# Spreading projections and VectorE chains around an attention's exponentials

## The chip, the cores and the metric

One core of a Trainium2 chip. The time is the device's time for one execution in microseconds (us). The runs came from more than one chip, so each kernel is judged by its ratio to the kernel before in the same rounds on the same chip: the mean time of one kernel's fast runs over that of the other's, so not quite the ratio of the medians quoted.

## The reference, cut to what matters

Two independent halves, put side by side in the output. Half B is attention with 32 heads of 20 over 2048 tokens:

```python
qkv = (x @ wqkv).reshape(B, S, 3, H, Dh)        # S = 2048, H = 32, Dh = 20
p = softmax(einsum("bhqd,bhkd->bhqk", q, k) * scale)
o = einsum("bhqk,bhkd->bhqd", p, v);  out_b = o.reshape(B, S, D) @ wo
```

Half A is a convolution over the sequence (an FFT in the reference, sums of small matmuls in the kernel):

```python
kv = shift_conv(k, 4 taps) * v
out_a = q * (long_conv(kv, ssm_k) + kv * ssm_D)
```

## The kernel before

The program is written as one loop of 512 steps: four passes over query chunks, eight groups of four heads, sixteen key blocks. A step exponentiates one block on ScalarE while TensorE makes the next scores:

```python
for b in range(NB):                 # 512
    EXP_task(b)                     # 2 ACTIVATEs of 128x1024 on ScalarE
    S_task(b + 1)                   # 4 score matmuls
    PV_task(b - 1)                  # 4 value matmuls
    budget = 1.0
    if b >= 24 and b % 5 == 0: kv_task(...)   # 8 VectorE instructions at once
    if lock is None: ...run_best()  # the task with the earliest deadline
    if nm == 0 and conv: ...        # else pieces of the convolution, up to the budget
```

Everything else is fitted in as tasks: K, Q and V projections, N (transpose and normalise one head group), T (transpose for the output projection) and O (output projection). After the first steps all of them, and the convolution, write one spare PSUM bank, MISC, which a VectorE cast must empty before the next may start. In these traces the instructions of an engine run in the order they were queued, so a task that waits holds back the scores queued after it. A "handover" is the stretch where a pass is over and its T and O tasks run.

```python
def kv_task(tb):                    # half A: shift convolution of one block
    P.op("dve", ... tA = k0 * C0)
    for j in range(1, KS):
        P.op("dve", ... tB = kj * Cj);  P.op("dve", ... tA = tA + tB)
    P.op("dve", ... kvst = tA * v)   # then two stores and the next load
...
add(b + 10, 0.35, ("N", qc, g), ...)
add(b0 + 12, 0.4, ("T", qc, qt), ...)             # all four T at once
add(b0 + 16 + 8 * qt + 4 * hf, 0.7, ("O", qc, qt, hf), ...)
# OnT_task(qt >= 2) first runs both O tasks of qt - 2
```

The softmax here doesn't subtract the row's maximum and nothing guards it: scores larger than these inputs give would overflow.

## Time and profile before

| | us |
|---|---|
| median of the three runs made before the prediction | 1092.08 |
| span of the profiled run | 1093.4 |
| first exponential starts | 16.87 |
| stream of 1024 exponentials at their pitch, the time from one to the next without a wait (1024 x 0.9175) | 939.5 |
| lost inside the stream | 121.9 |
| after the last exponential (1093.4-1078.27) | 15.1 |

The rows of ScalarE's timeline are start, duration, engine, line, what it does and how many were merged, and in brackets the idle time before the group with what ended it. A group's duration is about (count-1) times the pitch plus one full instruction of 1.0 us; what is missing between groups is what ScalarE waited. Every microsecond of wait in that stream lengthens the kernel by one. The prediction shows the lines.

### The profile page before, as it was taken

What the parts mean: (1) busy time and instruction counts of PE and PEld (TensorE: products, weight loads), DVE (VectorE), ACT (ScalarE), POOL (GpSimd) and SP (SyncE); (2) the same over time, 40 slices, a digit from 0 to 9 for tenths busy, and PEclk for the clock granted to TensorE, in tenths of its full rate; (3) what the DMA queues carried; (4) which work ended last, traced back from release to release, by engine and by line L of the source; (5) the groups of instructions that cost most, each with busy time, mean ns of one, the idle gap of its engine ahead of it and who ended that gap; (6) DMA issues with size and microseconds to landing.
All of it is one profiled execution on the core that took longest, in us unless ns stands there. A gap on an engine that the chain in (4) does not pass through costs nothing.

```text
span 1093.4 us, 24833 instructions
## 1 busy us (share of the span) xinstructions
PE 850.1 (78%) x11264; PEld 393.5 (36%) x11264; DVE 273.7 (25%) x558; ACT 953.2 (87%) x1027; POOL 118.8 (11%) x97
## 2 busy tenths in 40 slices
PE   5887777776668888888877889888888966666666
PEld 3322222221123555555544455555554411111112
DVE  3345554555102111111112440111112132000002
ACT  3786766669996999999979699999998899999994
POOL 3000000000310111222111011222110000000000
PEclk9998988886556999999988899999997865555556
DMA  9102222223823488888898497788885321000000
GB/s 340 38 32 85 85 85 85 85 82 100 134 45 92 117 199 177 193 180 180 181 194 184 136 239 173 178 185 191 175 182 132 83 73 49 1 1 1 1 1 25
DMA packets 74758, 129.04 MB, mean 118 GB/s; under 512 B 25730, under 2 KB 51452, under 8 KB 74652
## 3 DMA queue, kind: packets, MB, share of 16 engines
q1 hardware_dynamic: 71979, 124.09, 47.8%
q0 software_dynamic: 704, 2.74, 0.6%
q8 instruction: 88, 1.44, 0.6%
q10 hardware_dynamic: 1968, 0.61, 0.2%
q14 instruction: 19, 0.15, 0.1%
HBM read 116.81 MB, written 13.23 MB: 119 GB/s over the span
## 4 chain that ended last, share of the span: by engine, by line
ACT 62%; PE 23%; DVE 11%; DMA 2%; issue 1%; SPq 0%; ACTq 0%
ACT P_sb L419 62%; PE PS L306 7%; PE PS L407 4%; PE PS L584 3%; PE PS L503 3%; PE PS L432 3%; PE PS L325 2%; DVE KT L313 2%; DVE R L357 2%; DVE R L355 2%; DVE QT L313 1%; DVE V_sb L330 1%; DMA R<-in_B_wqkv_dram 1%; DVE OT_sb L440 1%; DMA R<-kv_scratch 1%
## 5 line engine op out<-in xcount | busy, mean ns | idle before, releaser
L419 ACT ACTIVATE P_sb<-PS 128x1024 bf16<-128x1024 f32 x1024 | 950.5, 1145 | 119.2 <-PE PS L407 112.6
L407 PE MATMUL PS<-QT,KT 20*128 20x512 bf16 x2048 | 240.5, 459 | 150.9 <-ACT P_sb L419 145.0
L432 PE MATMUL PS<-P_sb,V_sb 128*21 128x512 bf16 x2048 | 239.1, 459 | 1.2 <-ACT P_sb L419 1.2
L584 PE MATMUL PS<-R 128*128 128x128 bf16 (+15 forms) x5120 | 220.4, 196 | 6.1 <-DMA R<-kext_scratch 4.3
L584 PEld LDWEIGHTS PS<-R 128*128 128x128 bf16 x5120 | 197.2, 99 | 53.2 <-issue 48.7
L407 PEld LDWEIGHTS PS<-QT,KT 20*128 20x128 bf16 x2048 | 53.2, 94 | 301.0 <-ACT P_sb L419 254.4
L561 POOL COPY R<-R 32x512 bf16<-32x512 bf16 x80 | 106.7, 1333 | 417.7 <-PE PS L584 405.1
L306 PE MATMUL PS<-R 128*20 128x512 bf16 x1280 | 94.0, 430 | 37.1 <-DVE KT L313 11.1
L432 PEld LDWEIGHTS PS<-P_sb,V_sb 128*21 128x21 bf16 x2048 | 50.7, 90 | 153.7 <-issue 151.3
L440 DVE CAST OT_sb<-PS 128x512 bf16<-128x512 f32 x32 | 22.1, 691 | 273.6 <-PE PS L432 273.6
L597 DVE CAST ZH<-PS 128x256 bf16<-128x256 f32 x40 | 17.0, 424 | 289.3 <-PE PS L584 289.3
L306 PEld LDWEIGHTS PS<-R 128*20 128x20 bf16 x1280 | 29.9, 98 | 82.6 <-DVE QT L313 19.1
L503 PE MATMUL PS<-Wo_sb,OnT 128*128 128x320 bf16 x160 | 37.4, 388 | 7.3 <-DVE Bout L507 3.8
L325 PE MATMUL PS<-R 128*128 128x160 bf16 (+1 forms) x160 | 29.1, 316 | 13.7 <-DVE KT L313 5.8
L313 DVE CAST KT<-PS 128x512 bf16<-128x512 f32 x32 | 22.1, 690 | 44.5 <-PE PS L306 44.5
L313 DVE CAST QT<-PS 128x512 bf16<-128x512 f32 x32 | 22.1, 690 | 43.7 <-PE PS L306 43.7
L538 POOL MEMSET R<- 128x2048 bf16 x2 | 3.6, 1805 | 267.1 <-DMA kvr_scratch<-R 267.1
L503 PEld LDWEIGHTS PS<-Wo_sb,OnT 128*128 128x128 bf16 x160 | 16.6, 118 | 25.3 <-DVE Bout L507 9.1
L507 DVE CAST Bout<-PS 128x320 bf16<-128x320 f32 x32 | 15.7, 491 | 37.7 <-PE PS L503 37.2
L453 PE MATMUL PS<-ident,OT_sb 128*128 128x128 bf16 x128 | 14.7, 246 | 13.1 <-DVE OT_sb L440 12.8
L357 DVE TENSOR_TENSOR R<-R 128x640 bf16<-128x640 bf16 x48 | 23.6, 492 | 1.6
L355 DVE TENSOR_TENSOR R<-R 128x640 bf16<-128x640 bf16 x48 | 23.5, 490 | 1.1
(44 smaller groups left out, 239.4 us busy)
## 6 DMA issues: line engine op xcount, KB each, us to landing
R<-kext_scratch SPq DMA_DIRECT2D x320, 264.0 KB, 5.6
R<-in_A_k_dram SPq DMA_DIRECT2D x15, 640.0 KB, 3.9
R<-in_B_x_dram SPq DMA_DIRECT2D x4, 640.0 KB, 7.4
kext_scratch<-in_A_ssm_k_dram POOLq DMA_DIRECT2D x1, 2560.0 KB, 13.7
R<-in_A_v_dram SPq DMA_DIRECT2D x16, 160.0 KB, 5.4
kv_scratch<-R SPq DMA_DIRECT2D x16, 160.0 KB
kvr_scratch<-R SPq DMA_DIRECT2D x16, 160.0 KB
R<-kvr_scratch SPq DMA_DIRECT2D x8, 320.0 KB, 7.3
```

The source lines that it names most:

```text
L306: ins = e.matmul(bank[bk][32 * i:32 * i + DH, :], W_sb[:, cc, off + i * DH:off + (i + 1) * DH], xT[:, cc, c * 512:(c + 1) * 512], start=(c ...
L313: P.op("dve", lambda e: e.tensor_copy(dstT[:, g, c * 512:(c + 1) * 512], bank[bk]), reads=[bkb[bk]], writes=[bd])
L325: ins = e.matmul(bank[bk][:, 0:w], xT[:, cc, kb * 128:(kb + 1) * 128], W_sb[:, cc, 2 * D + h0 * DH:2 * D + h0 * DH + w], start=(cc == 0), ...
L355: P.op("dve", lambda e, j=j: e.tensor_tensor(tB, k[:, j, :], Ctile[:, j, :], ALU.mult), reads=[b_kst[i], b_C], writes=[b_tB])
L357: P.op("dve", lambda e: e.tensor_tensor(tA, tA, tB, ALU.add), reads=[b_tA, b_tB], writes=[b_tA])
L407: ins = e.matmul(bank[bk], KT[32 * u:32 * u + DH, g, kb * 128:(kb + 1) * 128], QT[32 * u:32 * u + DH, g, qc * 512:(qc + 1) * 512], start=T ...
L419: P.op("act", lambda e, pr=pr, s0=s0: e.activation(P_sb[:, pr % NPS, :], PS[:, s0 * 512:s0 * 512 + 1024], ACT.Exp, scale=scale), reads=[bk ...
L432: ins = e.matmul(bank[OBANK][32 * u:32 * u + DH + 1, :], V_sb[:, kb, 4 * g + u, :], P_sb[:, (2 * b + u // 2) % NPS, (u % 2) * 512:(u % 2) ...
L440: P.op("dve", lambda e: e.tensor_copy(OT_sb[:, i, :], bank[OBANK]), reads=[bkb[OBANK]], writes=[b_OT[i]])
L503: ins = e.matmul(bank[bk][:, 0:320], OnT[:, i, cc, :], Wo_sb[:, cc, hf * 320:(hf + 1) * 320], start=(cc == 0), stop=(cc == NCC - 1))
L561: P.op("pool", lambda e, dst=dst, src=src: e.tensor_copy(dst, src), reads=[cv["KVr"]], writes=[cv["KVX"][i]] if X == 3 else [], extra=(cv[ ...
L584: P.op("pe", lambda e, o=o, lhsT=lhsT, rhs=rhs, st=st, last=last: e.matmul(o, lhsT, rhs, start=st, stop=last, skip_group_check=True), read ...
```

## The change

Four things: the Q buffer shrinks to two query chunks, each projected one pass ahead (so x and Wq get a place of their own and outlive the first pass); the kv and output chains of half A become generators that queue two VectorE instructions a step; tasks and convolution draw on a running balance (0.9 a step, 1.4 in the first 24) instead of 1.0 reset each step; new deadlines for N, T and O. In the tail, casts alternate between VectorE and ScalarE.

```diff
-        QT = sb("QT", [128, NG, S])
+        QT = sb("QT", [128, 2, NG, 512])
...
+        xT = sb("xT", [128, NCC, S])
+        WQ = sb("WQ", [128, NCC, D])
         R = sb("R", [128, max(ph0, ph1)])     # holds WK, WV first, the convolution later
...
-                add(b + 10, 0.35, ("N", qc, g), lambda: N_task(qc, g))
+                add(b + 4, 0.35, ("N", qc, g), lambda: N_task(qc, g))
...
-                    add(b0 + 12, 0.4, ("T", qc, qt), ...)
+                    add(b0 + 5 + 4 * qt, 0.4, ("T", qc, qt), ...)
-                        add(b0 + 16 + 8 * qt + 4 * hf, 0.7, ("O", qc, qt, hf), ...)
+                        add(b0 + 6 + 4 * qt + hf, 0.75, ("O", qc, qt, hf), ...)
...
-            allx = b_xT + [b_Wa, b_Wb] + b_xst + ...   # what the convolution's loads wait for
+            allx = [b_Wa, b_Wb] + b_xst + ...
...
+            for qc in range(1, 4):
+                add(128 * (qc - 1) + 70 + 6 * g, 1.25, ("Q", g, qc), ...)
...
-            budget = 1.0
-            if b >= 24 and b % 5 == 0 and kv_next[0] < NKB:
-                kv_task(kv_next[0])
+            bal = min(bal + (1.4 if b < 24 else 0.9), 1.2)
+            if conv is None and kv_over and not any(e[3][0] in "XKV" for e in pend):
+                conv_setup()
+                conv = conv_iter()
...
+            if b >= 6:
+                micro(2)
```

V's second task (480 columns) is also cut into one of 160 and one of 320.

## The prediction

> **What bounds the kernel now.** I read the page first, then ScalarE's timeline, then VectorE, TensorE, GpSimd and SyncE in the stretches where ScalarE stands still.
>
> ```profile
> PE 850.1 (78%) x11264; PEld 393.5 (36%) x11264; DVE 273.7 (25%) x558; ACT 953.2 (87%) x1027; POOL 118.8 (11%) x97
> ...
> ACT  3786766669996999999979699999998899999994
> ...
> L419 ACT ACTIVATE P_sb<-PS 128x1024 bf16<-128x1024 f32 x1024 | 950.5, 1145 | 119.2 <-PE PS L407 112.6
> ```
>
> ScalarE is the bound: 1024 exponentials, and what it waits for is the score matmul (L407). The slices show where: tenths of 6 to 8 in the first nine slices, then nearly full with three dips. ScalarE's timeline has the pitch and the gaps (start, duration, merged count, idle before):
>
> ```profile
> 89.26 9.84 ACT L419 ACTIVATE P_sb<-PS 128x1024 bf16<-128x1024 f32 x10 [3.81 <-PE PS L407]
> ...
> 215.52 10.15 ACT L419 ACTIVATE P_sb<-PS 128x1024 bf16<-128x1024 f32 x10 [3.89 <-PE PS L407]
> 229.57 9.75 ACT L419 ACTIVATE P_sb<-PS 128x1024 bf16<-128x1024 f32 x10 [3.90 <-PE PS L407]
> ...
> 606.75 1.94 ACT L419 ACTIVATE P_sb<-PS 128x1024 bf16<-128x1024 f32 x2 [7.45 <-PE PS L407]
> ...
> 903.00 29.44 ACT L419 ACTIVATE P_sb<-PS 128x1024 bf16<-128x1024 f32 x32 [0.46 <-PE PS L407]
> ...
> 1052.50 25.77 ACT L419 ACTIVATE P_sb<-PS 128x1024 bf16<-128x1024 f32 x28 [0.46 <-PE PS L407]
> ```
>
> Pitch: (29.44-25.77)/4 = 0.9175 us, so a step (two exponentials) is 1.835 us and 1024 need 939.5 us. The stream runs from 16.87 to 1078.27 = 1061.4 us: it loses 121.9 us. By stage, start differences less count times pitch:
> - 16.87 to 66.21 (38 exponentials): 49.3-34.9 = 14.5
> - 66.21 to 247.18 (130): 181.0-119.3 = 61.7
> - first handover between passes (342 to 356): gaps of 3.90, 3.99, 0.40 = 8.3
> - 558 to 566: 4.79+0.89 = 5.7, TensorE waiting for a filter load
> - second handover: 7.45+2.85 = 10.3
> - third: 3.90+4.00+0.59+0.38 = 8.9
> - the rest, small gaps: 12.5
>
> The largest item is periodic: every fifth step a gap near 3.9 us. VectorE's timeline says why: at that step one kv block puts eight instructions into its queue.
>
> ```profile
> 95.39 0.48 DVE L352 TENSOR_TENSOR R<-R 128x640 bf16<-128x640 bf16 x1
> ...
> 98.93 0.49 DVE L358 TENSOR_TENSOR R<-R 128x640 bf16<-128x640 bf16 x1
> 99.34 0.68 DVE L313 CAST KT<-PS 128x512 bf16<-128x512 f32 x1
> ```
>
> The cast that frees the single spare PSUM bank stands behind 3.95 us of kv work; the next projection waits for the bank, and the scores stand behind that projection on TensorE. Then the array is cold: the K task after such a gap took 2.31 us (at 141.55) against 1.26 (at 150.13). Cost per block: spacing 14.05 us less five steps, 9.2, is 4.9 us; twelve or thirteen visible blocks give the 61.7. The last three or four blocks cost nothing: from 247 on no projection is left to hold up.
>
> **What the Trainium skill says.**
> 1. "TensorE: Matmul & The Clock Gate", Part 1 (HAM clock gate): half rate by default and after an idle window, full after about 3.4 us of activity. The trace agrees: granted clock 0.50 for all of 900 to 1060, where a step has only scores and value products; 1.00 while each step has a projection or convolution.
> 2. Same page, Part 4 (transpose): transposes don't count as busy in the same way. The clock fell from 0.98 to 0.50 at 594 to 596, after steps with transposes only: consistent, not proof.
> 3. Same page, "Architectural detail": ScalarE and VectorE are strict FIFO. The cast behind the kv block agrees.
> 4. "DMA: Bandwidth & Descriptors", Specifications: pieces under 512 B miss line rate. The kv gather has 160-byte rows; the DMA view gives about 150 GB/s for it and 215 to 243 for the filter loads after it.
>
> **The change, part by part.** I followed both scheduling loops and listed the tasks of each step (counts only). For the kernel before this gives the last projection at step 85 and the convolution's first piece at step 124, which fits 247 and 324 us. For the changed kernel: projections last until step 104, kv work is two VectorE instructions a step in steps 6 to 72, and the convolution runs from step 105 to 427.
>
> Total exponentials and TensorE work hardly change, so I price what the stream will lose.
>
> *Steps 0 to 23, 11 us.* Steps 0 to 2 still take six or so tasks each (the first gaps were 1.80, 1.39, 2.60, 0.73): 6.5. Steps 6 to 15 allow two tasks, now with about 1 us of kv work (2 x 0.49) ahead of the second task's bank release: about eight such steps at 0.6 = 4.5.
>
> *Steps 24 to 104, 8 us instead of some 62.* A K or Q step is 1.29 TensorE + 0.70 cast + gaps = 2.05 us, 0.21 over. The score matmul may be about 0.5 us late before ScalarE notices (0.92 less 0.40); 9.75 us for ten exponentials in a row of such steps, against 9.26, agrees. The new balance (0.9 a step, 1.25 a task) gives two such steps, then a lighter one: nothing lost. VectorE has 0.98 kv + 0.70 cast in 1.83 us, and they don't meet. kv loads: from a block's last instruction to the reload being ready took 6.86 us (255.59 to 262.45); two blocks are now 4.5 steps = 8.2 us apart: hidden. What I charge: in steps 15 to 40 many steps have just a 160-column V task (0.40+0.40+0.40 of 1.83), so the clock should fall; a K step is then 2.31+0.61+0.61 = 3.5, losing 1.4. Three of five K or Q tasks there: 4.2, plus 0.8; group ends, six at 0.5: 3.
>
> *Convolution start, a new wait, 19.5 us.* The setup's loads reuse the region that held the K and V weights, so they may start only when the last K task (step 104) is done, and the first convolution matmul is already in TensorE's queue one step later. Before, the same loads were released by the last kv store and had until 324:
>
> ```profile
> 282.48 5.57 SPq L144 DMA_DIRECT2D R<-kvr_scratch  x4
> ...
> 295.02 11.11 POOL L561 COPY R<-R 32x512 bf16<-32x512 bf16 x8 [8.85 <-DMA R<-kvr_scratch]
> ```
>
> 295.02-282.48 = 12.5, plus four of the eight copies (5.55): 18.1 us from release to the first operand. TensorE has one score and one value product in between, ScalarE about two steps: release at 1.9 us into step 104, scores out 20.3+1.7+0.6 later in that step's time, ScalarE dry at 4.6: 18. Restart on a cold array: 1.5 (0.90+0.54 before).
>
> *Handovers, 18 us instead of 27.5.* Before, deadlines put all four T ahead of the O tasks, and T2, T3 dragged two O each into one step (3.9 us gaps). The new ones interleave T, O, O, one a step: these bursts go. Steps of transposes still cool the array, and an O step at half clock is 0.61+0.61+1.51 = 2.7: 0.9 lost until the clock returns, about 3 a handover. The second also starts the first half's output chain: 8.1 us from load to data (issue 591.10, ready 599.24) still block VectorE, now one step earlier, ahead of the normalisation that the T tasks need; I get a 6.6 us gap, as the 7.45 before, and 3 more because each pair of tiles reloads in 3.5 us while its operations now come in half the time. So 3+12+3.
>
> *Unchanged:* the filter wait near 560, 5.7. *Rest:* 5 (waits of 0.46 at group ends only from step 428, small gaps of the convolution).
>
> Sum: 11+8+19.5+18+5.7+5 = 67.2, against 121.9: 54.7 less. The last 16 us gain about 1 from casts shared with ScalarE. 1092.1-55.7 = 1036.
>
> **The rivals.**
> (a) *The early loads hide the convolution start.* If the setup's waits didn't include the weight readers, its 19.5 would vanish: about 1017. Against it: the alias list keeps both weight buffers.
> (b) *Spreading leaves the array cold.* At half clock in most of steps 24 to 104, some 20 of 39 K and Q tasks lose 1.4 each: 28 instead of 5, about 1060. For it: the scores and value products alone stay at 0.50. Against: such a step fills TensorE (1.22+2.3), which brings the clock back, as at 328.
> (c) *VectorE becomes the bound early.* kv waits for its loads and blocks casts: up to 1.5 us for each of 14 blocks, about 1057. The 8.2 against 6.86 speaks against it.
> (d) *No gain: total TensorE work binds.* 850 us busy of 1093. Against it: a convolution step is 0.40+0.40+1.15 us and ran at the pitch (ten exponentials in 9.2 us) from 356 to 558. It would leave about 1090, and I see nothing for it.
>
> **Range and chances.** The terms that can be off are the convolution start (0 to 22), the cold array (2 to 28), and the second handover (6 to 18). Together: 1014 to 1060. Faster than 2% needs under 1070.2, where even (b) and (c) alone stop; together they would pass it.
>
> **What would show it.** Right: no periodic 3.9 us gaps before 210 us; one gap of 15 to 20 us near 230 (16.9 + 105 steps of 1.835 + the 19 lost by then = 228.6), TensorE waiting there for GpSimd's copy or the gather; clock dips to 0.5 before 100 us; no pairs of 3.9 us gaps at handovers, one gap of 6 us or so at the second with VectorE waiting for a load. Wrong: a convolution start without a gap, K tasks mostly at 2.3 us, VectorE waiting for k or v loads, or over 40 us lost before the convolution.

## The result

The changed kernel took 1042.34 us (1037.22 to 1044.18, 4 runs) against 1089.49 (1085.83 to 1097.8): ratio 0.955, 95% interval 0.948 to 0.962. Predicted: 1036, 1014 to 1060, "faster" at 0.95. A second measurement on another chip gave 0.953.

The page of the changed kernel, the same three lines as before (busy time by engine; ScalarE's busy tenths by slice; the exponentials with their idle time):

```profile
PE 815.2 (78%) x11344; PEld 393.6 (38%) x11344; DVE 266.9 (26%) x568; ACT 949.9 (91%) x1033; POOL 119.1 (11%) x97
...
ACT  3579999993999999999997999999999999999994
...
L427 ACT ACTIVATE P_sb<-PS 128x1024 bf16<-128x1024 f32 x1024 | 944.0, 1176 | 70.6 <-PE PS L415 67.4
```

The work is what it was; ScalarE's idle time before its exponentials fell from 119.2 to 70.6 us. The slices are full from the fourth on but for one 3 and one 7, and the beginning is worse than before (see the table). Its timeline:

```profile
31.86 7.44 ACT L427 ACTIVATE P_sb<-PS 128x1024 bf16<-128x1024 f32 x8 [2.51 <-PE PS L440]
44.01 3.80 ACT L427 ACTIVATE P_sb<-PS 128x1024 bf16<-128x1024 f32 x4 [4.71 <-PE PS L415]
...
72.61 22.15 ACT L427 ACTIVATE P_sb<-PS 128x1024 bf16<-128x1024 f32 x24 [0.49 <-PE PS L415]
...
229.50 12.99 ACT L427 ACTIVATE P_sb<-PS 128x1024 bf16<-128x1024 f32 x14 [1.07 <-PE PS L415]
258.58 1.94 ACT L427 ACTIVATE P_sb<-PS 128x1024 bf16<-128x1024 f32 x2 [16.09 <-PE PS L415]
...
277.63 123.29 ACT L427 ACTIVATE P_sb<-PS 128x1024 bf16<-128x1024 f32 x134 [0.58 <-PE PS L415]
...
559.99 1.94 ACT L427 ACTIVATE P_sb<-PS 128x1024 bf16<-128x1024 f32 x2 [6.00 <-PE PS L415]
...
997.32 25.77 ACT L427 ACTIVATE P_sb<-PS 128x1024 bf16<-128x1024 f32 x28 [0.47 <-PE PS L415]
```

The 3.9 us gaps at every fifth step are gone: after 72.61 groups run to 24, 28, 32 and 36 exponentials. There is one gap of 16.09 us at 242, one of 6.00 at 554, and no gap at the first handover (inside the group from 277.63). The stream runs from 17.75 to 1023.09 = 1005.3 us and loses 65.8. By stage, with the pitch of before (the first two rows of before are cut at the 48th exponential, as those of after are; the prediction cut them at the 38th, 14.5 and 61.7):

| stretch | before, lost | predicted | after, lost |
|---|---|---|---|
| steps 0 to 23 | 16.6 | 11 | 21.8 |
| to the convolution's start | 59.6 (to step 83) | 8 | 6.4 |
| convolution's start | 1.4 | 19.5 | 18.2 |
| three handovers | 27.5 | 3+12+3 | 0, 6.6, 0.5 |
| filter load near 560 | 5.7 | 5.7 | none over 1.2 |
| rest | 11.1 | 5 | 12.3 |
| sum | 121.9 | 67.2 | 65.8 |

(Steps 0 to 23 are 48 exponentials, 17.75 to about 83.6: 65.9 less 44.0. The next 152 up to 229.50: 145.9 less 139.5. The convolution's start: 16.09+0.26+1.26+0.58.)

The one large gap, in the timeline of all engines (GpSimd's clearing, SyncE's issue of the gather, GpSimd's copies, the first convolution matmuls):

```profile
239.84 3.67 POOL L550 MEMSET R<- 128x2048 bf16 x2 [224.54 <-PE PS L309]
239.89 5.72 SPq L144 DMA_DIRECT2D R<-kvr_scratch  x4
...
250.71 11.07 POOL L573 COPY R<-R 32x512 bf16<-32x512 bf16 x8 [7.19 <-DMA R<-kvr_scratch]
...
256.26 1.73 PE L596 MATMUL PS<-R 128*128 128x128 bf16 x21 [15.73 <-POOL R L573]
```

The clearing and the loads were released by the last projection matmul (L309). The first operand was there 256.26-239.89 = 16.4 us after that, TensorE stood for 15.73 of it, and ScalarE for 16.09.

### The profile page after: what moved, and what is told of

The parts are those of the page before. It is cut to its first block, busy times and chain, and to the rows that moved or that the text cites. A ratio compares the mean times of both kernels' runs of the same rounds, so it can differ in the third digit from the quotient of the medians.

```text
span 1040.8 us, 25021 instructions
## 1 busy us (share of the span) xinstructions
PE 815.2 (78%) x11344; PEld 393.6 (38%) x11344; DVE 266.9 (26%) x568; ACT 949.9 (91%) x1033; POOL 119.1 (11%) x97
## 4 chain that ended last, share of the span: by engine, by line
ACT 76%; PE 15%; DVE 4%; DMA 2%; issue 1%; SPq 1%; POOL 1%; ACTq 0%
ACT P_sb L427 76%; PE PS L309 4%; PE PS L415 4%; PE PS L440 2%; PE PS L596 2%; PE PS L516 1%; PE PS L329 1%; DVE OT_sb L448 1%; DMA R<-in_B_wqkv_dram 1%; PE PS L461 1%; DMA R<-kvr_scratch 1%; DMA R<-kv_scratch 1%; SPq L144 1%; POOL R L573 1%; PE PS L289 0%
## 5 line engine op out<-in xcount | busy, mean ns | idle before, releaser
L427 ACT ACTIVATE P_sb<-PS 128x1024 bf16<-128x1024 f32 x1024 | 944.0, 1176 | 70.6 <-PE PS L415 67.4
L415 PE MATMUL PS<-QT,KT 20*128 20x512 bf16 x2048 | 227.3, 434 | 159.4 <-ACT P_sb L427 146.8
L596 PE MATMUL PS<-R 128*128 128x128 bf16 (+15 forms) x5120 | 219.8, 195 | 18.4 <-POOL R L573 15.7
L440 PE MATMUL PS<-P_sb,V_sb 128*21 128x512 bf16 x2048 | 226.4, 434 | 1.8 <-ACT P_sb L427 1.2
L309 PE MATMUL PS<-xT,WQ 128*20 128x512 bf16 x640 | 49.1, 445 | 1.3 <-DVE O_norm L469 0.4
L309 PE MATMUL PS<-xT,R 128*20 128x512 bf16 x640 | 44.4, 411 | 6.1 <-DMA R<-in_B_wqkv_dram 4.1
L329 PE MATMUL PS<-R,xT 128*128 128x160 bf16 (+1 forms) x240 | 34.4, 285 | 2.7 <-DVE V_sb L334 1.4
L516 PE MATMUL PS<-Wo_sb,OnT 128*128 128x320 bf16 x160 | 30.0, 328 | 3.4 <-DVE OnT L507 1.8
L329 PEld LDWEIGHTS PS<-R,xT 128*128 128x128 bf16 x240 | 19.5, 108 | 18.7 <-DVE KT L317 4.4
L623 DVE CAST R<-PS 128x256 bf16<-128x256 f32 x40 | 17.0, 425 | 32.1 <-PE PS L617 32.1
L309 PEld LDWEIGHTS PS<-xT,WQ 128*20 128x20 bf16 x640 | 16.5, 100 | 22.8 <-issue 7.0
L309 PEld LDWEIGHTS PS<-xT,R 128*20 128x20 bf16 x640 | 15.6, 95 | 24.8 <-issue 8.0
```

The source lines that it names most:

```text
L309: ins = e.matmul(bank[bk][32 * i:32 * i + DH, :], Wt[:, cc, off + i * DH:off + (i + 1) * DH], xT[:, cc, c * 512:(c + 1) * 512], start=(cc ...
L329: ins = e.matmul(bank[bk][:, 0:w], xT[:, cc, kb * 128:(kb + 1) * 128], WKV[:, cc, D + h0 * DH:D + h0 * DH + w], start=(cc == 0), stop=(cc ...
L415: ins = e.matmul(bank[bk], KT[32 * u:32 * u + DH, g, kb * 128:(kb + 1) * 128], QT[32 * u:32 * u + DH, qc % 2, g, :], start=True, stop=True ...
L427: P.op("act", lambda e, pr=pr, s0=s0: e.activation(P_sb[:, pr % NPS, :], PS[:, s0 * 512:s0 * 512 + 1024], ACT.Exp, scale=scale), reads=[bk ...
L440: ins = e.matmul(bank[OBANK][32 * u:32 * u + DH + 1, :], V_sb[:, kb, 4 * g + u, :], P_sb[:, (2 * b + u // 2) % NPS, (u % 2) * 512:(u % 2) ...
L516: ins = e.matmul(bank[bk][:, 0:320], OnT[:, i, cc, :], Wo_sb[:, cc, hf * 320:(hf + 1) * 320], start=(cc == 0), stop=(cc == NCC - 1))
```

## The experiments

Eleven runs of nine new kernels: b_kvsplit_dl2 and after_again repeat one on another chip. A line number in an experiment's profile can be shifted against the two kernels above.

### b_kvsplit: the kv split alone, on the kernel before

```diff
-            if b >= 24 and b % 5 == 0 and kv_next[0] < NKB:
-                kv_task(kv_next[0])
+            if b >= 24:                 # kv_task yields after each VectorE instruction
+                for _ in range(2):
+                    next(kv, None)
```

> The kernel before with one part of the change alone: the kv block's eight VectorE instructions go in two a step from step 24 on instead of eight at once every fifth step; projections, deadlines and buffers stay as before. My theory (the casts queued behind the kv block made most of the first quarter's loss): the 3.9 us gaps go, the 61.7 us lost from 66 to 247 us fall to about 10, and the time is about 1040 us (1089.5 less 50), with the pairs of 3.9 us gaps at the handovers still there. Rival (the gain comes from spreading the projections and from the Q tasks moved out of the first pass): a projection in every step still overloads TensorE, little changes, 1070 to 1085 us.

Measured: 1054.24 us (1054.2 to 1054.67), ratio 0.9625 (0.9606 to 0.9643). ScalarE's timeline of this kernel:

```profile
137.21 30.63 ACT L428 ACTIVATE P_sb<-PS 128x1024 bf16<-128x1024 f32 x30 [1.15 <-PE PS L416]
...
307.83 1.94 ACT L428 ACTIVATE P_sb<-PS 128x1024 bf16<-128x1024 f32 x2 [3.90 <-PE PS L416]
313.76 1.94 ACT L428 ACTIVATE P_sb<-PS 128x1024 bf16<-128x1024 f32 x2 [4.00 <-PE PS L416]
```

The periodic gaps are gone and the handover's pair is still there. This one part gives 41 us of the kernel's 1095, so most of the gain. My 1040 was too low: thirty exponentials took 30.63 us where the pitch makes 27.6 (29 x 0.9175+1.0), so fifteen projections in a row cost 0.2 us a step in small waits. From 67.94 to 234.46 it lost 21.5 us where I had allowed 10. Neither side was right in full: the kv blocks carry most, and the evenly loaded steps of the changed kernel are worth some 13 us more (from the 48th to the 200th exponential it loses 6.5 us, this one 19.4).

### a_kvwhole: the changed kernel with kv in groups of eight again

```diff
             if b >= 6:
-                micro(2)
+                if kv_over:
+                    micro(2)
+                elif b % 4 == 1:
+                    micro(8)
```

> The changed kernel with the kv work put back into groups of eight VectorE instructions, one group every fourth step; all else of the change kept. My theory: sixteen gaps of 3 to 4 us come back before 150 us, plus cold-array K tasks after each: 1042 plus 50 to 65 us, about 1095 us. Rival (the balance leaves so many light steps that a group mostly meets one): plus 5 to 15 us, about 1052 us.

Measured: 1080.78 us (1076.27 to 1085.67), ratio 0.987 (0.983 to 0.990): 37 us more than the changed kernel on the same chip (after_again, 0.953). Its timeline has gaps at every fourth step again, most of 1.8 to 3.2 us rather than 3.9 (the longest after the start 5.89, at 122 us):

```profile
182.29 1.94 ACT L427 ACTIVATE P_sb<-PS 128x1024 bf16<-128x1024 f32 x2 [3.09 <-PE PS L415]
...
200.76 1.94 ACT L427 ACTIVATE P_sb<-PS 128x1024 bf16<-128x1024 f32 x2 [2.31 <-PE PS L415]
```

The cause is confirmed from the other side; the size lies between the two expectations, perhaps because among spread tasks a group sometimes meets a light step (not looked at).

### a_olddl: the changed kernel with the old deadlines

```diff
-add(b + 4, 0.35, ("N", ...   add(b0 + 5 + 4 * qt, 0.4, ("T", ...   add(b0 + 6 + 4 * qt + hf, 0.75, ("O", ...
+add(b + 10, 0.35, ("N", ...  add(b0 + 12, 0.4, ("T", ...           add(b0 + 16 + 8 * qt + 4 * hf, 0.75, ("O", ...
```

> The changed kernel with the deadlines of the N, T and O tasks of before (all T first, O 4 steps apart); all else of the change kept. My theory: T2 and T3 again pull two O tasks each into one step, two gaps near 3.9 us at each of three handovers: plus 15 to 25 us, about 1062 us. Rival (the handovers became cheap because the array now stays warm through them, not because of the order): the bursts run warm and cost at most 2 us each, plus 4 to 8 us, about 1048 us.

Measured: 1069.78 us (1068.57 to 1071.73), ratio 0.977 (0.975 to 0.979): 26 us more than the changed kernel on the same chip (after_again). The third handover of this kernel:

```profile
818.76 1.94 ACT L427 ACTIVATE P_sb<-PS 128x1024 bf16<-128x1024 f32 x2 [3.90 <-PE PS L415]
824.70 1.94 ACT L427 ACTIVATE P_sb<-PS 128x1024 bf16<-128x1024 f32 x2 [4.00 <-PE PS L415]
```

The same pair as in the kernel before. The first handover shows 3.90 and 2.85, the second 6.29, 2.55, 3.00, 2.85, 1.98. So the deadlines are worth 26 us in the changed kernel, against 37 for the kv split; on the kernel before they are worth less (see b_kvsplit_dl). The deadline of N moved with those of T and O and was not tried alone.

### a_convlate: the convolution's first piece 13 steps after its loads

```diff
                 conv_setup()
                 conv = conv_iter()
+                conv_at = b + 13
...
-            if nm == 0 and conv is not None and not conv_over:
+            if nm == 0 and conv is not None and not conv_over and b >= conv_at:
```

> The changed kernel, but the first convolution piece is queued on TensorE 13 steps after the setup's loads instead of in the same step. My theory: the 16.1 us gap near 242 us goes, nothing takes its place because the convolution ended 84 steps before the end: about 1026 us (1042 less 16). Rival (the array goes cold in the 13 empty steps and the delay is given back at the end or at the handovers): less than 5 us gained, 1037 to 1042 us.

Measured: 1044.47 us (1038.07 to 1048.34), ratio 0.9546 (0.9516 to 0.9576), the changed kernel on the same chip 0.9532: nothing gained. The 16 us gap is gone from its timeline, but three others are larger or new:

```profile
528.52 1.94 ACT L427 ACTIVATE P_sb<-PS 128x1024 bf16<-128x1024 f32 x2 [5.45 <-PE PS L415]
...
595.57 5.11 ACT L427 ACTIVATE P_sb<-PS 128x1024 bf16<-128x1024 f32 x5 [5.54 <-PE PS L415]
...
610.80 1.94 ACT L427 ACTIVATE P_sb<-PS 128x1024 bf16<-128x1024 f32 x2 [7.38 <-PE PS L415]
```

At 528 TensorE had waited 5.08 us for a filter load, at 595 5.13 us for VectorE to empty the value bank, at 610 6.60 us for the normalisation. In the last two VectorE stood in its queue at the output chain's first instruction, waiting for a kv load (7.48 and 6.32 us). In the changed kernel that chain starts on the second handover, where the convolution pauses; 13 steps later it starts beside the convolution. The first load is waited for as long as before (7.48 us against 7.56), but now a cast and a normalisation that running work needs stand behind such waits. The gain was given back to a wait that lay elsewhere, not to the cold array that my rival named. New gaps of 18.4 less the 6.6 of before make 11.8 of the 16; the rest isn't resolved (the profiled run is the fastest of its four, with a beginning 6.8 us luckier than that of the changed kernel).

### b_kvsplit_dl, b_kvsplit_dl2: the kv split and the deadlines, on the kernel before

The edit is b_kvsplit's plus the new deadlines; the second run is the same kernel beside the changed one.

> The kernel before with two small parts of the change: kv work two instructions a step (as in b_kvsplit, 1054 us) and the new deadlines of the N, T and O tasks; Q still all in the first pass, full Q buffer, old budget. Theory (Q one pass ahead and the balance bring nothing here beyond what these two bring; they trade evenly loaded steps for the convolution's late start): two 3.9 us gaps at each of three handovers go, about 20 us less than b_kvsplit, 1030 to 1038 us, so below the changed kernel's 1042. Rival (the balance and the Q tasks moved out are worth 10 us or more): 1046 to 1054 us.

> The same kernel as b_kvsplit_dl (kv work in single steps and new deadlines on the kernel before), beside the changed kernel on one chip. Theory (Q one pass ahead and the balance bring nothing beyond those two parts): equal or faster than after_again, 0 to 8 us. Rival (they are worth 10 us or more): slower than after_again by that much.

Measured: 1040.74 us (1038.39 to 1045.97), ratio 0.9497 (0.947 to 0.953); beside the changed kernel 1041.19 us (1036.14 to 1046.01), ratio 0.9505 (0.947 to 0.954) against 0.9532 (0.951 to 0.956). The two can't be told apart. Q one pass ahead and the balance together bring nothing net: what they earn in the projections (some 13 us) they pay at the convolution's start (18.2 against 1.4). They were not tried one without the other. The 1030 to 1038 us of the expectation were missed: the deadlines added 13 us to the kv split on one chip (0.9625 less 0.9505) and not 20, because the second handover still lost 8 to 10 us and the tail grew from 14.1 to 17.6.

### after_again: the changed kernel once more

> The changed kernel again, as an anchor on the chip of these runs (the first measurement came from another chip). If the clock's phase in steps 3 to 14 is chance, single runs spread over some 8 us (1037 to 1047); the ratio to before stays 0.955 within 0.004.

Measured: 1043.56 us (1040.48 to 1046.04), ratio 0.9532 (0.9506 to 0.9558), spread 5.6 us. Five profiles, this one among them, have the same instructions queued for the first 28 exponentials; they lost 21.0 (the changed kernel), 20.4 (a_olddl), 18.3 (a_aone), 17.5 (after_again) and 14.2 us (a_convlate) in them. That is chance, by how long the clock stayed low: the mean granted clock from 30 to 62 us was, in the same order, 0.57, 0.57, 0.73, 0.73 and 0.89.

### a_nobank: no debt after step 2

```diff
             bal = min(bal + (1.4 if b < 24 else 0.9), 1.2)
+            if b == 3:
+                bal = 0.9
```

> The changed kernel with the balance reset at step 3, so the debt of steps 0 to 2 no longer leaves steps 3 to 5 without a task. Theory (three steps of scores and value products alone let the granted clock fall to 0.5, and the paired V tasks with 0.42 us waits between keep it there until 61 us): the clock stays near 1.0 from 20 to 64 us, the first 28 exponentials lose 10 to 13 us instead of 21.0, and the time is 6 to 9 us less than the changed kernel's (ratio to before near 0.949). Rival (the early loss is the casts' waits behind the kv instructions, not the clock): no change beyond 2 us.

Measured: 1031.31 us (1029.01 to 1033.34), ratio 0.9396 (0.9378 to 0.9413). Stretches of 10 us, first of the changed kernel, then of this one (busy time and count by engine, granted clock, DMA share, GB/s):

```profile
core 0: us, PE busy (x) PEld busy (x) DVE busy (x) ACT busy (x) POOL busy (x), PEclk, DMA share, GB/s
30.00:40.00 10.00, 6.82 (x64) 2.56 (x61) 1.69 (x6) 7.44 (x8) 0.00 (x0) 0.74 0.17 52
40.00:50.00 10.00, 8.55 (x64) 3.33 (x64) 4.42 (x11) 4.80 (x6) 0.00 (x0) 0.50 0.23 79
50.00:60.00 10.00, 8.74 (x70) 3.16 (x71) 3.78 (x9) 4.82 (x6) 0.00 (x0) 0.50 0.02 6
```

```profile
40.00:50.00 10.00, 8.00 (x113) 3.32 (x112) 6.29 (x15) 7.93 (x9) 0.00 (x0) 1.00 0.25 84
50.00:60.00 10.00, 8.63 (x121) 3.71 (x113) 7.37 (x18) 9.22 (x10) 0.00 (x0) 1.00 0.37 116
```

TensorE is as busy in both (8.5 and 8.7 against 8.0 and 8.6 us of 10) and does little more than half as much in the first: 134 matmuls in 20 us at clock 0.50 against 234 at 1.00. The first 28 exponentials lose 11.1 us instead of 21.0, and the kv instructions are still there, so the rival falls. The reset also gives steps 3 to 5 tasks to do, so this is not the clock alone; for the clock alone see the five profiles above. The time fell by more than expected, 15 us by the ratios (1.4% of 1095, across two chips). The two profiled runs differ by 9.3 us, so a part of the 15 isn't placed; the steps that follow also lose less, 3.0 us from 62.78 to 214.42.

### a_aone: the output chain one instruction a step, five steps after its loads

```diff
             A_load(B, 0)
             A_load(B, 1)
+            for _ in range(5):
+                yield
...
-                micro(2)
+                micro(1 if kv_over else 2)
```

> The changed kernel with the output chain's VectorE instructions one a step instead of two, and first five steps after its first loads are issued. Theory (VectorE stands in its FIFO on the first load, 7.6 us, with the normalisation for the T task behind it): the 6.0 us gap at the second handover goes, 5 to 6 us less, ratio to before near 0.950, and no load waits over 1 us on VectorE's multiplication by D. Rival (the handover pays anyway, on a cold array): less than 2 us.

Measured: 1035.56 us (1034.34 to 1037.35), ratio 0.9445 (0.9427 to 0.9462). The 6 us gap at the second handover is gone; from 517.32 a single group of 188 exponentials runs through it. The gain is some 9 us by the ratios. The two profiled runs differ by 8.3 us: 6.6 for that gap, 2.7 for a luckier beginning, and 1.0 lost elsewhere. One of my signs was wrong: VectorE still waited up to 6.4 us for single loads (15.5 us in all). At the second handover the chain's first multiplication (at 557.35) no longer waited and no longer stood ahead of the normalisation. The edit slows the chain and delays it at once; which of the two is needed was not tried.

### a_nolate and a_best: the three repairs, without and with the later convolution

a_nolate is a_nobank and a_aone together, and in the last pass all T tasks first again; a_best adds a_convlate's delay.

```diff
-                    add(b0 + 5 + 4 * qt, 0.4, ("T", qc, qt), ...)
+                    add(b0 + (5 + 4 * qt if qc < 3 else 5), 0.4, ("T", qc, qt), ...)
```

> a_best without the 13 steps' delay of the convolution (balance reset, output chain one a step and late, T tasks first in the tail): what the delay is worth once the output chain is out of the way. Theory: the 16 us gap near 225 us is back and little else changes, 13 to 16 us more than a_best's 1012, about 1026. Rival (the delay is given back here too, as in a_convlate): within 4 us of a_best.

> The changed kernel with the balance reset, the output chain one instruction a step and five steps late, the convolution's first piece 13 steps after its loads (a_convlate), and in the last pass all T tasks first. Theory (in a_convlate the 16 us saved came back as 5.5 us for a filter load and 5.5 and 7.4 us behind the output chain's loads; with that chain out of the way most of the 16 stays saved): 16 less 5.5, plus 7 early, plus 6 of the output chain, plus 2.8 in the tail: about 26 us less than the changed kernel, 1016 us, ratio 0.93. Rival (waiting moves on again: the output chain now runs beside the convolution and its loads are late there): 1030 to 1036 us.

Measured: a_nolate 1023.13 us (1013.89 to 1027.68), ratio 0.9326 (0.9282 to 0.937), with a gap of 15.68 us at the convolution's start; a_best 1011.86 us (1010.0 to 1015.46), ratio 0.9231 (0.9208 to 0.9254). So the delay that was worth nothing alone is worth about 10 us here (0.95% of 1095; the two intervals lie 0.3% apart at the nearest), across two chips; I had expected 13 to 16. In a_best the largest wait after the start is 1.28 us; from 253.95 its timeline has

```profile
253.95 185.74 ACT L427 ACTIVATE P_sb<-PS 128x1024 bf16<-128x1024 f32 x202 [0.51 <-PE PS L415]
```

202 exponentials in one group, with the convolution and the first handover inside. Its stream loses 38 us (17.91 to 995.55, less 939.5). a_best beats both kernels: 7.7% less than the kernel before, and 3.2% less than the changed one by the two ratios.

## Why the prediction was right, and where its terms were off

The mechanism and the sum were right: 67.2 us lost predicted, 65.8 found. Step by step:

- **The kv blocks.** Named as the largest item, shown by b_kvsplit (41 us alone) and a_kvwhole (37 us back). For the stretch to the convolution 8 us were predicted, 6.4 found. "They don't meet" and "hidden" held: no wait of VectorE for k or v loads is in the profile's waits.
- **The convolution's start.** 19.5 predicted, 18.2 found, with the wait on GpSimd's copy as described. It took 16.4 us from release to operand instead of 18.1.
- **Steps 0 to 23.** The term that was mis-sized: "11 us" measured 21.8. I saw that the V steps could cool the array and charged that only for steps 15 to 40. I didn't see that the debt of steps 0 to 2 leaves steps 3 to 5 with no task, so the clock fell at 35 us and not at step 15; until 62 us the two V tasks and the K task of a step then ran at half rate (a K task 2.31 us). a_nobank and the five profiles under after_again show it. What I put down to kv instructions ahead of the second cast was small: the waits there are 0.42 us, with or without kv.
- **The handovers.** The bursts went, as a_olddl shows; the cold array there cost little: 0 and 0.5 us instead of 3 each. It did not vanish. From the first T to the last O the mean granted clock was 0.78 to 1.00 in the thirty handovers of the ten profiles with the new order (1.00 in five of them; in the first handover 1.00 in the changed kernel, 0.84 in after_again), against 0.55 to 0.72 in the six of the kernel before and b_kvsplit (a_olddl, whose balance spreads the old order over 56 to 71 us, has 0.76 to 0.92). Order and bursts went together, so which of them warmed the array isn't separated. The second handover lost 6.6, as the gap's own working said, without the 3 for reloads and 3 for the clock. VectorE's timeline there (the output chain's first instruction, and the normalisation behind it):

```profile
556.91 0.49 DVE L641 TENSOR_TENSOR R<-R,Dbc 128x640 bf16<-128x640 bf16 x1 [7.56 <-DMA R<-kv_scratch]
...
558.13 0.49 DVE L469 TENSOR_TENSOR O_norm<-PS,rden 128x320 bf16<-128x320 bf16 x1
```

- **The filter wait.** I called it unchanged; it was gone. In the changed kernel three Q tasks interrupt the convolution while the second half's gather loads (steps 225 to 234 by the task lists), which would give the filter loads time; a_convlate, where the convolution stands elsewhere against those tasks, has a wait of 5.45 us again. That fits but wasn't tried by itself, so it stays argued.
- **The rest.** 12.3 instead of 5: among them gaps of 1.19 at 433, 1.18 at 485 and 1.18 at 700 us. Each follows a Q task between pieces of the convolution that ran at half clock, two of them:

```profile
430.33 2.35 PE L309 MATMUL PS<-xT,WQ 128*20 128x512 bf16 x20
...
696.94 2.31 PE L309 MATMUL PS<-xT,WQ 128*20 128x512 bf16 x20 [0.23 <-DVE O_norm L469]
```

The third, at 482.15, took 2.31 us too; a warm one takes 1.26. Steps with little or no convolution come before each, and the clock fell in them. So moving Q out of the first pass isn't free: I charged no cold array in this stretch.

- **The tail.** I took 1 us off; it grew from 15.1 to 17.7 us. The interleaved T and O order, good for the handovers, makes a chain of the last one. TensorE's first T of the tail, before and after:

```profile
1081.22 1.25 PE L488 MATMUL PS<-ident,O_norm 128*128 128x128 bf16 x10 [0.88 <-DVE O_norm L461]
```

```profile
1026.05 0.71 PE L496 MATMUL PS<-ident,O_norm 128*128 128x128 bf16 x5 [0.88 <-DVE O_norm L469]
```

Before, two T ran back to back (10 transposes) and hid each other's copy; now one runs, and TensorE waits for its copy. a_olddl, with the old order and the shared casts, has a tail of 14.9 (1066.7-1051.78), so the order costs 2.8. Sharing the casts shows no gain: the new order without it has 17.7 and 17.6 us (b_kvsplit_dl, b_kvsplit_dl2), the old order without it 15.1 and 14.1 (the kernel before, b_kvsplit).

I had predicted 10.8 us too little at the beginning, 7.3 too little in the rest and 3.6 too little in the tail (1 us less predicted, 2.6 more found), against 10.9 too much for the handovers, 5.7 for the filter wait and 2.9 for the two well-sized terms. The closeness of 1036 to 1042 owes something to that.

Three readings in the prediction need a correction. The clock of the kernel before was not 1.00 in every step with a projection or convolution: from 89.26 to 103 us its mean was 0.87. The 0.50 from 900 to 1060 us is no plain agreement with the page either, since TensorE was busy for 102 of these 160 us and not idle. And two sums are off by 0.3 us, in opposite directions (8 x 0.6 is 4.8, 1.9+18.1 is 20.0).

Of the rivals, (a) was false for this kernel. (b) was false for steps 24 to 104, where three K and Q tasks ran at half rate (at 92.6, 164.9 and 226.6 us) and not 20, but true for steps 3 to 14. (c) and (d) were false.

## What to carry to other kernels

When one engine sets the pace, price each wait in its stream by stretch; a chain of cheap instructions on an idle engine can be the largest item, if something that the pacing engine needs stands behind it in the queue. A load that is waited for inside such a queue should be issued some steps before its first use, and starting a phase earlier was worth nothing here, because its loads could not start earlier too. Removing one wait can only move it (a_convlate): find what it will collide with, clear that as well, and measure the pair.

## What the Trainium skill lacked or had wrong

- "TensorE: Matmul & The Clock Gate", Part 1, ties the half rate to an idle window and the full rate to about 3.4 us of activity. No window of the changed kernel near 35 us was idle: from 32 to 36 us TensorE was busy for 2.11 of 4 us, with 0.4 us of scores and 0.61 us of value products in each 1.83 us, and the clock fell; it stayed at 0.50 from 36 to 62 us while the profile's TensorE was 85% busy. How much activity counts as busy is missing on the page.
- The same page, Part 4, says that transposes don't count as busy in the same way. No run here tests that alone, since steps with only scores and value products sit at 0.50 too (900 to 1060 us of the kernel before). A handover with the transposes together had a mean clock of 0.55 to 0.72, one with O tasks between them 0.78 to 1.00; the page doesn't say how much other work is enough.
- The same page, Part 1, says that the ramp costs under 1% of a typical kernel and depends on where the window falls. The chance agrees: the same queued instructions lost 14.2 to 21.0 us, and the difference, 6.8 us, is 0.7% of the kernel and as much as some of the effects studied here. The cost of the ramp by itself was not measured.
- No page has the cost of a phase change in one number. Here it was 16.4 to 18.1 us from the release of a 1.3 MB gather in 160-byte rows to the first matmul operand, GpSimd's copies of 5.5 us included.
